# Early rows from six groups, weight loads in the attention's buffers, doubled branch hints and earlier gather conditions in a fused attention and mixture-of-experts kernel

## Chip, cores, metric

The kernel runs on one core of a Trainium2 chip. The metric is the time of one execution in device microseconds (us). Names of engines are those of the profile: PE multiplies matrices, DVE, ACT and POOL work on vectors, SP issues transfers; PEld is PE's weight load.

## The reference

Three stages follow each other. 3072 tokens of 384 numbers each (4 x 768 positions, 8 heads of 48) go through a linear attention with a decaying state; a feed-forward layer of width 2048 with a leaky ReLU follows; then a second mixture of experts, where a token whose skip score is positive goes to the one of 8 experts with the largest logit:

```python
def _moe_ref(x, w_in, w_out):
    h = x @ w_in
    g = np.maximum(0.01 * h, h)
    return (g @ w_out).astype(np.float32)

def _moe2_ref(x, w_skip, w_gate, w1, w2):
    do_compute = x @ w_skip > 0
    out = x.copy()
    xc = x[do_compute]
    logits = xc @ w_gate
    e_idx = np.argmax(logits, axis=1)
    ...                                   # gate_w: softmax weight of the chosen expert
    for e in range(E):
        mask = e_idx == e
        h = np.maximum(xc[mask] @ w1[e], 0.0)
        y[mask] = gate_w[mask, None] * (h @ w2[e])
    out[do_compute] = xc + y
```

How many tokens an expert gets depends on the data: 13, 424, 67, 318, 34, 229, 22 and 69 of experts 0 to 7 here. The kernel works in blocks of 128, so expert 1 has four blocks, expert 3 three, expert 5 two, all others one: 14 blocks.

## The kernel before, in words

Every product is made of three half-precision products (high by high, high by low, low by high part).

**First feed-forward layer.** 3072 tokens are eight groups of 384 (three tiles of 128). For each group the first matmul (`mm1`, L470 to L472) runs over f = 0 to 15, each f giving 128 of the 2048 hidden numbers; ACT and DVE (L475, L476, L485, L486) make the activation and its two halves. Then the second matmul (`mm2`, L498 to L500) makes the output of three tiles. Beside the matmuls of a group the generator `routing` of the group before is advanced at chosen values of f: logits, choice, position of each token in its expert's list, and three scatters by POOL (L592) that write token numbers into three lists in memory, `idxl`. `store_x` writes the finished rows into `xbuf`, from which experts gather them.

**Last group.** The largest expert, E0 = 1, begins early: a first block of 128 of its tokens, the early block, is gathered before all tokens are counted. `early_list` clears the block's buffer, loads the first 128 entries of the three lists (`early_l`, L635, issued by SP), takes the minimum on DVE (L639), gathers the rows by POOL (L653) and transposes them by a transfer of SP (L667). In the last group it runs at f = 7, 8, 11 and 14, the gather limited to rows of the first seven groups. After the last f the attention's pools are closed, buffers `xg` are cleared by POOL (L881) and eight pieces of expert 2's weights, 384 KB each, are loaded (`load_expert`, L691) into `wb`. Pieces are split into halves by ACT and DVE (L188, L189) while the second matmul runs. `counts` reads the counts and the lists back (`h<-idxl`), takes their minimum (L610, L611), transposes it on PE (L615), and puts the counts into registers.

**Experts.** The early block is computed first, then experts 0 to 7. A block is `hidden` (72 short matmuls, L972 to L974, with L978 and L979 on ACT and DVE) and `combine` (24 matmuls of 384 columns, L986 to L988, y on DVE L990, and a scatter into the output by POOL L993). Block j > 0 of an expert stands under a condition on its count (L1071), nested, so that the first block that isn't needed is jumped over with all behind it. Every engine has its own copy of these branches. `announce` places hints for such a branch ahead of it (L1158): for the other engines at the start of a block, for PE after `hidden`. At the start of an expert e stand conditions around the gathers of its further blocks (L1032, L1034) and of the next expert's block 1 (L1041); before expert 1's remaining blocks these are L1037 and L1041. PE executes the branch of each condition, with nothing in it.

Instructions of an engine run in the order in which they stand in its queue.

Of the kernel before, what the change touches and what calls it, by code (L numbers as in the profile page):

```python
# [18 lines left out]
P = 128  # L19
# [5 lines left out]
ST = 128  # L25
# [30 lines left out]
NBLK = 4  # L56


@with_exitstack
def kernel(ctx: ExitStack, tc: tile.TileContext, rk, nat, wT, uN, w_in, w_out, wsg,  # L60
# [15 lines left out]
    raw = ph1.enter_context(tc.tile_pool(name="raw", bufs=3))  # L76
# [39 lines left out]
    def att_load():  # L116
        i = state["loads"]
        assert i < 3 or done["r"] > i - 3
        state["loads"] += 1
        rkt = raw.tile([112, 2, NPAIR, ST], F32, name="rkt")  # L120
        nt = raw.tile([P, 3, 2, NPAIR, D], F32, name="nt")
        sp.dma_start(rkt, rk[i])
        sp.dma_start(nt, nat[i])
        steps[i] = (rkt, nt)

    pw = cst.tile([112, 7, 2, NPAIR], F32, name="pw")
# [496 lines left out]
    def early_list():  # L625
# [14 lines left out]
        gather(E0, 0, None, idx, NT - GT)  # L640
# [193 lines left out]

    rts = iter(())
# [5 lines left out]
    for g in range(NG):  # L841
# [11 lines left out]
        if g > 1:  # L853
            for f in range(NF):
# [7 lines left out]
                if f in ((2, 4, 6) if last else (3, 6, 9)):  # L862
                    next(rts, None)
                if f == (7 if last else 12):
                    for i in range(TPG):
                        store_x(g - 1, i)
                if last and f == 7:
                    firsts = early_list()
                if last and f in (8, 11, 14):
                    next(firsts)  # L870
        if last:
# [4 lines left out]
            w_b = [m2p.tile([P, 768], F32, name=f"wb{i}") for i in range(NW)]  # L876
# [10 lines left out]
            later = [(e, c) for e in range(2, E) for c in range(8)]  # L887
            parts = [load_expert(*later.pop(0), w_b, NW) for _ in range(8)]

            def load_pieces(n):  # L890
                for _ in range(min(n, len(later))):
                    parts.append(load_expert(*later.pop(0), w_b, NW))

            def split_pieces(n, more=True):
                for _ in range(min(n, len(parts))):
                    parts.pop(0)()
                    if more and not state["hold"]:
                        load_pieces(1)
# [59 lines left out]
    def fetch(e, j, k=None, ix=None):  # L958
        gather(e, j, k, ix)
        turn_rows(e, j, k)  # L960

    def hidden(e, k, par, hset, cuts=(0, 0)):
# [3 lines left out]
        for b in range(2):  # L966
# [12 lines left out]
            v.scalar_tensor_tensor(hl, hp, 0.0, hh, op0=ALU.max, op1=ALU.subtract)  # L979

# [32 lines left out]

    def passage():
        turn_here(0, 0, bank[0])
        next(cnts)
        with tc.If(rv[E0] > P):
            fetch(E0, 1)
        with tc.If(rv[0] > P):
            fetch(0, 1)  # L1020
        state["hold"] = False
        load_pieces(4)
# [7 lines left out]
    for e in range(E):  # L1030
        if e != E0:
            with tc.If(rv[e] > 2 * P):  # L1032
                fetch(e, 2)
                with tc.If(rv[e] > 3 * P):  # L1034
                    fetch(e, 3)
        else:
            with tc.If(rv[e] > 3 * P):  # L1037
                fetch(e, 3)
        if e + 1 < E:
            k = 2 if e + 1 == E0 else 1  # L1040
            with tc.If(rv[e + 1] > k * P):  # L1041
                fetch(e + 1, k)
        odd = 1 if e == E0 else 0
        if e == E0:
            fetch_ahead(e + 2)
            split_pieces(sum(PIECES[e + 1]))
        else:
            announce(e, 1)
            cuts = PIECES[e + 1]
            hidden(e, buf_of(e, 0), e % 2, e % 2, cuts[:2])  # L1050
            split_pieces(cuts[2])
            announce(e, 1, ENGINES[:1])
            combine(e, buf_of(e, 0), e % 2, idx_t[:, 0, e:e + 1], lambda: fetch_ahead(e + 2))
        st = ExitStack()
        for j in range(1, NBLK):
            st.enter_context(tc.If(rv[e] > j * P, label=f"e{e}b{j}"))
            announce(e, j + 1)
            hidden(e, buf_of(e, j), (e + j + odd) % 2, 2 if j % 2 else e % 2)
# [103 lines left out]
```

## Time and profile before

| | |
|---|---|
| runs | 662.57, 663.7, 666.19 us |
| median | 663.7 us |
| profiled execution, its own time | 667.2 us |
| its span, first to last instruction | 665.4 us |
| mean granted PE clock | 0.974 |
| PE busy | 613.0 us, 92% of the span |
| DVE, ACT, POOL busy | 422.6, 256.7, 251.4 us |

PE is busy nearly throughout, so the time is read from the gaps between its matmuls: the list of waits says how long, and for whom; the timeline of an engine gives start, duration, operation and, in brackets, the idle time before it and what ended that. Records of branches and hints carry a q behind the engine's name, as PEldq, and belong to its sequencer.

### The profile page before, as it was taken

The page shows a single profiled execution, that of the slowest core. Times are in us where ns is not written, and L with a number is a line of the kernel's source. Part 1 is how long each engine was busy: PE and PEld are TensorE (multiplying, and loading weights), DVE is VectorE, ACT ScalarE, POOL GpSimd, SP SyncE. Part 2 cuts the span into 40 slices and gives each one's busy share as a digit, 9 for nine tenths or more (in the row PEclk, how much of TensorE's full clock was granted, in tenths as well). Part 3 has the DMA queues.
Part 4 walks back from the last instruction along what each step waited for, and adds up shares of the span by engine and source line. Part 5 has one row for each costly group of instructions (what it writes and reads, how often), then busy time and mean ns, then how long its engine had stood idle before and what let it go on. Part 6 is the DMA issues. An engine that isn't in the chain of part 4 may idle for free.

```text
span 665.4 us, 17739 instructions
## 1 busy us (share of the span) xinstructions
PE 613.0 (92%) x7198; PEld 408.5 (61%) x7198; DVE 422.6 (64%) x917; ACT 256.7 (39%) x539; POOL 251.4 (38%) x242
## 2 busy tenths in 40 slices
PE   8879988889999999999999999999969889897984
PEld 5656655556666666666666665665645767675763
DVE  7899988954289469838957934841755362643751
ACT  1225756552144236324434512531534341432530
POOL 2857664443545442633544543110233112311200
PEclk9889999999999999999999999999999899997987
DMA  8757354613626542652642530031239397394740
GB/s 277 219 165 214 82 185 135 184 65 73 168 77 143 158 152 81 159 175 81 140 146 76 112 116 18 2 84 34 72 93 316 108 243 199 91 279 109 209 102 11
DMA packets 60351, 89.06 MB, mean 134 GB/s; under 512 B 20706, under 2 KB 44224, under 8 KB 60240
## 3 DMA queue, kind: packets, MB, share of 16 engines
q1 hardware_dynamic: 56784, 81.64, 43.5%
q0 software_dynamic: 2880, 5.49, 2.8%
q8 instruction: 67, 1.10, 0.7%
q14 instruction: 44, 0.36, 0.2%
q10 hardware_dynamic: 576, 0.47, 0.2%
HBM read 68.86 MB, written 17.23 MB: 129 GB/s over the span
## 4 chain that ended last, share of the span: by engine, by line
PE 41%; DMA 19%; issue 18%; DVE 12%; POOL 5%; ACT 2%; SPq 0%; POOLq 0%; ACTq 0%; DVEq 0%
DMA out_x<-y,idx 10%; PE bank L498 6%; PE bank L500 6%; PE bank L499 6%; DMA idxl<-tokid,su 5%; PE bank L470 5%; PE bank L472 5%; PE bank L471 5%; DMA out_x<-y,early_i 3%; PE bank L399 2%; DVE gg L476 2%; DVE wc L207 2%; PE bank L351 1%; PE bank L327 1%; DVE bank L199 1%
## 5 line engine op out<-in xcount | busy, mean ns | idle before, releaser
L470 PE MATMUL bank<-xt,slotA 128*128 128x384 f16 x384 | 126.0, 328 | 2.4 <-DVE gg L476 2.3
L471 PE MATMUL bank<-xt,slotA 128*128 128x384 f16 x384 | 125.7, 327 | 0.0
L472 PE MATMUL bank<-xt,slotA 128*128 128x384 f16 x384 | 125.7, 327 | 0.0
L498 PE MATMUL bank<-slotB,slotC 128*128 128x393 f16 (+1 forms) x336 | 111.4, 332 | 0.0
L499 PE MATMUL bank<-slotB,slotC 128*128 128x393 f16 (+1 forms) x336 | 111.1, 331 | 0.0
L500 PE MATMUL bank<-slotB,slotC 128*128 128x393 f16 (+1 forms) x336 | 111.1, 331 | 0.0
L476 DVE TENSOR_TENSOR gg<-bank,gg 128x384 f32<-128x384 f32 x128 | 70.0, 549 | 28.7 <-ACT gg L475 28.2
L475 ACT ACTIVATE gg<-bank 128x384 f32<-128x384 f32 x128 | 62.1, 490 | 49.4 <-PE bank L472 46.1
L486 DVE TENSOR_TENSOR slotC<-gg,slotC 128x384 f16<-128x384 f32 x101 | 77.7, 773 | 0.2
L291 POOL TENSOR_TENSOR dg<-cs,diag 128x512 f32<-128x512 f32 x21 | 22.2, 1059 | 132.0 <-DVE cs L284 132.0
L485 ACT CAST slotC<-gg 128x384 f16<-128x384 f32 x112 | 56.8, 508 | 25.3 <-DVE gg L476 25.3
L526 DVE SCALAR_TENSOR_TENSOR x<-bank,x 128x384 f16<-128x384 f32 x24 | 13.2, 556 | 69.6 <-ACT x L523 68.4
L263 POOL TENSOR_TENSOR rkt<-rkt,consts 112x512 f32<-112x512 f32 x44 | 56.9, 1318 | 0.0
L592 POOL DMA_INDIRECT idxl<-tokid,su x24 | 25.5, 1063 | 75.8 <-DVE su L589 65.7
L471 PEld LDWEIGHTS <-slotA 128*128 128x128 f16 x384 | 37.7, 98 | 25.2 <-issue 3.4
L472 PEld LDWEIGHTS <-slotA 128*128 128x128 f16 x384 | 37.7, 98 | 25.2 <-issue 0.5
L470 PEld LDWEIGHTS <-slotA 128*128 128x128 f16 x384 | 37.6, 98 | 24.0 <-issue 0.3
L522 ACT ACTIVATE x<-bank 128x384 f16<-128x384 f32 x24 | 11.8, 492 | 93.2 <-PE bank L500 75.2
L500 PEld LDWEIGHTS <-slotC 128*128 128x128 f16 x336 | 33.1, 98 | 23.2 <-issue 0.7
L498 PEld LDWEIGHTS <-slotC 128*128 128x128 f16 x336 | 33.0, 98 | 22.2 <-issue 0.5
L499 PEld LDWEIGHTS <-slotC 128*128 128x128 f16 x336 | 33.0, 98 | 21.0 <-issue 0.5
L978 ACT ACTIVATE h<-bank 128x512 f16<-128x512 f32 x28 | 16.7, 596 | 72.9 <-PE bank L974 60.6
(213 smaller groups left out, 1319.9 us busy)
## 6 DMA issues: line engine op xcount, KB each, us to landing
wb<-in_w SPq DMA_DIRECT2D x48, 384.0 KB, 6.9
nt<-in_nat SPq DMA_DIRECT2D x24, 576.0 KB, 5.8
rkt<-in_rk SPq DMA_DIRECT2D x24, 448.0 KB, 3.9
xbuf<-x SPq DMA_DIRECT2D x23, 384.5 KB, 4.4
wst<-in_w_in SPq DMA_DIRECT2D x16, 384.0 KB, 9.4
wst<-in_w_out SPq DMA_DIRECT2D x16, 384.0 KB, 3.2
wst<-in_w SPq DMA_DIRECT2D x16, 384.0 KB, 8.0
out_x<-x SPq DMA_DIRECT2D x24, 192.0 KB
```

Source lines behind the costliest of these rows:

```text
L263: eng.tensor_mul(r4[:, a], r4[:, a], tab.unsqueeze(2).broadcast_to([112, NPAIR, 2, C]))
L470: pe.matmul(ph[:, :n], wh, xt[:, 0, k, t0:t0 + n], start=k == 0, stop=False)
L471: pe.matmul(ph[:, :n], wh, xt[:, 1, k, t0:t0 + n], start=False, stop=False)
L472: pe.matmul(ph[:, :n], wl, xt[:, 0, k, t0:t0 + n], start=False, stop=k == NK - 1)
L475: act.activation(gg[:, :n], ph[:, :n], AF.Copy, scale=0.01)
L476: v.tensor_max(gg[:, :n], ph[:, :n], gg[:, :n])
L485: act.copy(gT[:, 0, f, t0:t0 + n], gg[:, :n])
L486: eng.tensor_sub(gT[:, 1, f, t0:t0 + n], gg[:, :n], gT[:, 0, f, t0:t0 + n])
L498: pe.matmul(po[:, :c1 - c0], gh, w_out_s[:, 0, f, c0:c1], start=start, stop=False)
L499: pe.matmul(po[:, :c1 - c0], gh, w_out_s[:, 1, f, c0:c1], start=False, stop=False)
L500: pe.matmul(po[:, :c1 - c0], gl, w_out_s[:, 0, f, c0:c1], start=False, stop=stop)
L592: g_.indirect_dma_start(out=idxl[i], out_offset=bass.IndirectOffsetOnAxis(ap=su[:, i:i + 1], axis=0), in_=tokid[:, ti:ti + 1], in_offset=N ...
```

## The change

1. The attention's input buffers become one lasting tile `raw`; after the attention its slices serve as the weight buffers `w_b`. `load_pieces(1)` stands at every odd f of the last group, and the eight loads after the last f are gone.
2. `early_list` starts at f = 0 of the last group, with steps at f = 1, 3 and 6; the gather is limited to the rows of the first six groups. Steps of `routing` and `store_x` of the group before stand at the same f as in the other groups (3, 6, 9 and 12 instead of 2, 4, 6 and 7).
3. The conditions for the gathers of an expert's blocks 1 and 2 form `fetch_more(e)`. It stands in block 0 of the expert before, between `hidden` and `combine`; for expert 2 it stands ahead of expert 1's block 1, and for the experts 1 and 0 in `passage` of the early block. Block 3's condition stands at the start of block 1.
4. PE's hint is placed twice: after the first half of `hidden` and after `hidden`.

```diff
+RAW = 2 * NPAIR * (ST + 3 * D)
...
-        rkt = raw.tile([112, 2, NPAIR, ST], F32, name="rkt")
-        nt = raw.tile([P, 3, 2, NPAIR, D], F32, name="nt")
+        b = i % 3 * RAW
+        rkt = raw[:112, b:b + 2 * NPAIR * ST].rearrange("p (x a t) -> p x a t", x=2, t=ST)
+        nt = raw[:, b + 2 * NPAIR * ST:b + RAW].rearrange("p (k q a d) -> p k q a d", k=3, q=2, d=D)
...
+    raw = cst.tile([P, 3 * RAW], F32, name="raw")
...
-        gather(E0, 0, None, idx, NT - GT)
+        gather(E0, 0, None, idx, NT - 2 * GT)
...
+    w_b = [raw[:, i * 768:(i + 1) * 768] for i in range(NW)]
...
-                if f in ((2, 4, 6) if last else (3, 6, 9)):
+                if f in (3, 6, 9):
                     next(rts, None)
-                if f == (7 if last else 12):
+                if f == 12:
                     for i in range(TPG):
                         store_x(g - 1, i)
-                if last and f == 7:
+                if last and f == 0:
+                    assert done["r"] == NST
                     firsts = early_list()
-                if last and f in (8, 11, 14):
+                if last and f in (1, 3, 6):
                     next(firsts)
+                if last and f % 2:
+                    load_pieces(1)
...
-            w_b = [m2p.tile([P, 768], F32, name=f"wb{i}") for i in range(NW)]
...
-            parts = [load_expert(*later.pop(0), w_b, NW) for _ in range(8)]
...
+            if between and b == 0:
+                between()
...
+    def fetch_more(e):
+        with tc.If(rv[e] > P):
+            fetch(e, 1)
+            with tc.If(rv[e] > 2 * P):
+                fetch(e, 2)
...
-        with tc.If(rv[E0] > P):
-            fetch(E0, 1)
-        with tc.If(rv[0] > P):
-            fetch(0, 1)
+        fetch_more(E0)
+        fetch_more(0)
...
-        if e != E0:
-            with tc.If(rv[e] > 2 * P):
-                fetch(e, 2)
-                with tc.If(rv[e] > 3 * P):
-                    fetch(e, 3)
-        else:
-            with tc.If(rv[e] > 3 * P):
-                fetch(e, 3)
-        if e + 1 < E:
-            k = 2 if e + 1 == E0 else 1
-            with tc.If(rv[e + 1] > k * P):
-                fetch(e + 1, k)
...
         if e == E0:
+            fetch_more(e + 1)
             fetch_ahead(e + 2)
...
-            hidden(e, buf_of(e, 0), e % 2, e % 2, cuts[:2])
+            hidden(e, buf_of(e, 0), e % 2, e % 2, cuts[:2], lambda: announce(e, 1, ENGINES[:1]))
             split_pieces(cuts[2])
             announce(e, 1, ENGINES[:1])
+            if e + 1 < E and e + 1 != E0:
+                fetch_more(e + 1)
...
+            if j == 1:
+                with tc.If(rv[e] > 3 * P):
+                    fetch(e, 3)
             announce(e, j + 1)
-            hidden(e, buf_of(e, j), (e + j + odd) % 2, 2 if j % 2 else e % 2)
+            hidden(e, buf_of(e, j), (e + j + odd) % 2, 2 if j % 2 else e % 2, (0, 0),
+                   lambda: announce(e, j + 1, ENGINES[:1]))
             announce(e, j + 1, ENGINES[:1])
```

Three places show where instructions stand. The first is SP's queue in the last group: `out_x<-x` are the previous group's output rows, `xbuf<-x` its rows for the experts, `consts<-consts` the transpose of the early block. Before:

```order
L534 DMA out_x<-x_6179 128x384
L541 DMA xbuf<-x_6056 128x769
L541 DMA xbuf<-x_6137 128x769
L541 DMA xbuf<-x_6179 128x769
L635 DMA early_l<-idxl_58 128x1
L635 DMA early_l<-idxl_59 128x1
L635 DMA early_l<-idxl_60 128x1
L667 DMA_TRANSPOSE consts<-consts 128x6x128
L691 DMA wb_6563<-in_w 128x3x256
```

Now:

```order
L536 DMA out_x<-x_6129 128x384
L637 DMA early_l<-idxl_58 128x1
L637 DMA early_l<-idxl_59 128x1
L637 DMA early_l<-idxl_60 128x1
L693 DMA raw<-in_w 128x3x256 x3
L669 DMA_TRANSPOSE consts<-consts 128x6x128
L693 DMA raw<-in_w 128x3x256
L693 DMA raw<-in_w 128x768 x2
L543 DMA xbuf<-x_6006 128x769
L543 DMA xbuf<-x_6087 128x769
L543 DMA xbuf<-x_6129 128x769
```

The list loads and six of eight weight loads stand ahead of the previous group's rows for the experts.

The second is PE's queue from the last matmul of expert 1 to the first of expert 2. Before:

```order
L988 MATMUL bank_95<-slotE,h_6593 128x384
L1064 REGISTER_ALU
L1064 COMPARE_AND_BRANCH
L1064 UNCONDITIONAL_BRANCH
L1061 UNCONDITIONAL_BRANCH
L1071 UNCONDITIONAL_BRANCH x3
L1032 COMPARE_AND_BRANCH
L1034 COMPARE_AND_BRANCH
L1034 UNCONDITIONAL_BRANCH x2
L1032 UNCONDITIONAL_BRANCH
L1041 COMPARE_AND_BRANCH
L1041 UNCONDITIONAL_BRANCH x2
```

Now (L1078 is the condition that was L1071, L1068 the one that was L1061):

```order
L996 MATMUL bank_92<-slotE,h_6542 128x384
L1071 REGISTER_ALU
L1071 COMPARE_AND_BRANCH
L1071 UNCONDITIONAL_BRANCH
L1068 UNCONDITIONAL_BRANCH
L1078 UNCONDITIONAL_BRANCH x3
L978 LDWEIGHTS slotA
```

The conditions for gathers are gone from this place. They stand, as L1023 and L1025, in PE's queue between the hidden layer (L978 to L980 now) and the second matmul (L994) of a block 0, here of expert 2, with the second of the two hints (L1165) ahead of them. Now:

```order
L980 MATMUL bank_90<-xT_6521,slotA 128x128
L1018 ISA
L1165 BRANCH_PREFETCH_HINT
L1023 COMPARE_AND_BRANCH
L1025 COMPARE_AND_BRANCH
L1025 UNCONDITIONAL_BRANCH x2
L1023 UNCONDITIONAL_BRANCH
L994 LDWEIGHTS h_6541
```

The third is PE's queue around the hints for the exit of expert 3, in its last block. Before, the hint stands behind the hidden layer and 24 matmuls ahead of the branch L1071:

```order
L974 MATMUL bank_93<-xT_6578,slotA 128x128
L1010 ISA
L1158 BRANCH_PREFETCH_HINT
L986 LDWEIGHTS h_6592
```

Now both hints stand in the middle of the hidden layer, since nothing holds the second one back:

```order
L980 MATMUL bank_85<-xT_6536,slotA 128x128
L1018 ISA
L1165 BRANCH_PREFETCH_HINT
L978 LDWEIGHTS slotA
L978 MATMUL bank_86<-xT_6536,slotA 128x128
L1165 BRANCH_PREFETCH_HINT
```

The hints stand half a hidden layer, 36 matmuls, further ahead of the branch.

## Rows read from the trace of the kernel before

**Rows 1.** Waits of PE over the span: engine, line, waited for; us in total, times, longest

```profile
PE bank L972 <- PEq L1071: 9.7, 5, 4.9
...
PE bank L569 <- DVE oh L563: 3.5, 1, 3.5
PE bank L972 <- DMA xT<-xg: 3.2, 1, 3.2
...
PE bank L232 <- DVE slotC L486: 2.2, 1, 2.2
...
PE bank L615 <- DVE x L525: 1.0, 1, 1.0
...
PE bank L972 <- DVE xT L663: 0.8, 1, 0.8
```

**Rows 2.** Timeline of DVE, 474 to 498: start, us, line, operation, [idle before]

```profile
481.56 0.55 DVE L486 TENSOR_TENSOR slotC<-gg,slotC 128x384 f16<-128x384 f32 x1
486.47 0.16 DVE L639 TENSOR_REDUCE early_i<-early_l 128x1 uint32<-128x3 uint32 x1 [4.36 <-DMA early_l<-idxl]
...
492.44 3.47 DVE L813 TENSOR_SCALAR lg<-lg 128x27 f32<-128x27 f32 x1
```

**Rows 3.** Timeline of POOL in the same stretch

```profile
491.74 4.14 POOL L881 MEMSET xg<- 128x769 f32 x6 [3.25 <-issue]
```

**Rows 4.** Waits of SP's queue, 460 to 660

```profile
SPq L635 <- DMA idxl<-tokid,su: 6.1, 2, 5.6
```

**Rows 5.** Timeline of DVE, 498 to 535

```profile
519.10 0.68 DVE L611 TENSOR_TENSOR h<-h 8x512 f32<-8x512 uint32 x1 [0.94 <-DMA h<-idxl]
```

**Rows 6.** Windows: us; busy of PE, PEld, DVE, ACT, POOL; clock, DMA share, GB/s

```profile
461.00:485.00 24.00, 24.00 (x213) 15.16 (x211) 14.94 (x47) 12.64 (x29) 3.67 (x4) 1.00 0.19 58
498.00:520.00 22.00, 20.98 (x121) 12.12 (x119) 11.46 (x27) 8.90 (x14) 5.59 (x6) 0.93 0.89 277
```

**Rows 7.** Branch L1071 on PE's sequencer, exits of experts 0, 2, 3, 5: ns min/median/max, start

```profile
L1071 PEldq COMPARE_BRANCH  x1: 4391/4391/4391, 537.8 to 537.8; - x1
...
L1071 PEldq COMPARE_BRANCH  x1: 1398/1398/1398, 574.0 to 574.0; - x1
...
L1071 PEldq COMPARE_BRANCH  x1: 6180/6180/6180, 600.3 to 600.3; - x1
...
L1071 PEldq COMPARE_BRANCH  x1: 3911/3911/3911, 632.9 to 632.9; - x1
```

**Rows 8.** Hints on PE's sequencer, experts 2 and 3

```profile
L1158 PEldq BRANCH_PREFETCH_HINT  x1: 35/35/35, 571.4 to 571.4; - x1
...
L1158 PEldq BRANCH_PREFETCH_HINT  x1: 35/35/35, 597.7 to 597.7; - x1
```

**Rows 9.** Timeline of PE, first matmul of experts 2, 3, 4, 6, 7

```profile
568.26 0.23 PE L972 MATMUL bank<-xT,slotA 128*128 128x128 f16 x1 [1.07 <-DVEq L1061]
...
577.45 0.23 PE L972 MATMUL bank<-consts,slotB 128*128 128x128 f16 x1 [1.09 <-PEq L1071]
...
607.54 0.29 PE L972 MATMUL bank<-xT,slotC 128*128 128x128 f16 x1 [4.90 <-PEq L1071]
...
637.76 0.29 PE L972 MATMUL bank<-xT,slotE 128*128 128x128 f16 x1 [2.55 <-PEq L1071]
...
647.77 0.23 PE L972 MATMUL bank<-consts,slotA 128*128 128x128 f16 x1 [0.47 <-PEq L1071]
```

**Rows 10.** Gather conditions on PE's sequencer over the span: ns min/median/max, first and last

```profile
L1032 PEldq COMPARE_BRANCH  x7: 70/217/337, 530.3 to 647.5; - x7
...
L1041 PEldq COMPARE_BRANCH  x10: 70/186/214, 530.7 to 637.5; - x10
```

**Rows 11.** Windows, columns as in rows 6

```profile
607.60:613.50 5.90, 5.90 (x57) 5.90 (x58) 1.18 (x2) 1.33 (x2) 1.04 (x1) 0.50 0.17 53
637.40:640.80 3.40, 3.04 (x29) 3.04 (x30) 1.32 (x2) 0.00 (x0) 0.00 (x0) 0.50 0.29 75
```

**Rows 12.** The page's DMA queues: packets, MB, share

```profile
q8 instruction: 67, 1.10, 0.7%
```

More of the change, by code (lines that the diff above doesn't have):

```diff
@@ L75 @@
     stg = ph1.enter_context(tc.tile_pool(name="stg", bufs=2))
-    raw = ph1.enter_context(tc.tile_pool(name="raw", bufs=3))
     att = ph1.enter_context(tc.tile_pool(name="att", bufs=2))
@@ L833, in first_logits, with load_pieces, split_pieces @@
         take_logits(0, pl, 1.0 / (SX * SR))
+    w_b = [raw[:, i * 768:(i + 1) * 768] for i in range(NW)]
+    later = [(e, c) for e in range(2, E) for c in range(8)]
+    parts = []
+    def load_pieces(n):
+        for _ in range(min(n, len(later))):
+            parts.append(load_expert(*later.pop(0), w_b, NW))
+    def split_pieces(n, more=True):
+        for _ in range(min(n, len(parts))):
+            parts.pop(0)()
+            if more and not state["hold"]:
+                load_pieces(1)
     rts = iter(())
@@ L861 @@
                     late_logits(g, gT, f - 3, bank[3])
-                if f in ((2, 4, 6) if last else (3, 6, 9)):
+                if f in (3, 6, 9):
                     next(rts, None)
-                if f == (7 if last else 12):
+                if f == 12:
                     for i in range(TPG):
                         store_x(g - 1, i)
-                if last and f == 7:
+                if last and f == 0:
+                    assert done["r"] == NST
                     firsts = early_list()
-                if last and f in (8, 11, 14):
+                if last and f in (1, 3, 6):
                     next(firsts)
+                if last and f % 2:
+                    load_pieces(1)
         if last:
@@ L886 @@
             y_b = [m2p.tile([P, DM], F32, name=f"y{i}") for i in range(2)]
-            later = [(e, c) for e in range(2, E) for c in range(8)]
-            parts = [load_expert(*later.pop(0), w_b, NW) for _ in range(8)]
[L890 to L898, printed above, removed]
         if g == 0:
@@ L960, in fetch, with hidden @@
         turn_rows(e, j, k)
-    def hidden(e, k, par, hset, cuts=(0, 0)):
+    def hidden(e, k, par, hset, cuts=(0, 0), between=None):
         w1s, _ = ev[e % len(ev)]
```

## The prediction

> **What bounds the kernel now.** I read three things in order: which engine is always occupied, what interrupts it, and what the interruptions wait for. PE is the engine; the list of its waits [rows 1] names every idle time that matters behind the attention part. Six entries of it lie in the region that the diff touches: 2.2 us before L232 at the end of the last first layer, 3.5 us before L569 shortly after, 1.0 us before L615, 0.8 us behind L663, and then, between experts, 9.7 us in five waits put down to PE's own sequencer and 3.2 us put down to xT. So the end of the kernel is PE's work plus these gaps, and the change is worth what it takes out of them. Half-speed stretches of PE's clock come on top: two of them [rows 11] hold 5.90 and 3.04 us of PE work at a granted 0.50, which at full speed would be 2.95 and 1.52 us.
>
> The 2.2 us: DVE finishes L486 at 481.56 + 0.55 and then stands 4.36 us before L639, the minimum over the three lists, waiting for the early_l loads [rows 2]. Everything of the running first layer is queued behind L639 on DVE. SP in its turn had waited 5.6 us at L635 for the scatter into idxl [rows 4]. PE runs on from banks that are full already and feels 2.2 of the 4.36.
>
> The 3.5 us are another thing: the tiny scaling L813 took 3.47 us [rows 2] while POOL cleared six xg buffers in 4.14 us from 491.74 [rows 3]. Both stand in the changed program where they stood, so I leave this gap alone.
>
> The gaps between experts: every exit is a branch that jumps over blocks not needed, and the sequencer's record says how long each took [rows 7]: 1.4 us at the end of expert 2, but 4.39 at expert 0, 6.18 at expert 3 and 3.91 at expert 5. The sequencer runs ahead of the matmuls, so 1.4 us disappears and the larger ones don't: PE stood 4.90 us before expert 4 and 2.55 before expert 6 [rows 9], and 3.2 before expert 1 [rows 1]. (Expert 0's is put down to the transfer of xT by the inference of the view; its 4.39 us branch ends at 542.2, two us after the last matmul, and carries it.) Where the branch came in time there is still 1.07, 1.09 and 0.47 us [rows 9]: after the jump PE's sequencer works through the conditions for the next gathers, of which PE executes nothing: 0.07 to 0.34 us each, medians 0.217 at L1032 and 0.186 at L1041 [rows 10].
>
> **The change part by part. Early list.** Its loads now come at f = 1, directly behind the previous group's output stores, and read lists that the group before that had finished; the scatter that SP waited for has left the path. L639 moves up to f = 3, two steps of the loop behind its loads. Of the 4.36 us that DVE stood, most was the scatter that SP had waited for [rows 2, 4]; what is left is the loads' own way. What is queued behind the minimum on DVE is the same chain of L476 and L486, so a late load would cost there what it costs now; I see none. The rows of the last two groups are outside the early gather's bound, and the gather and the transpose leave from f = 3 and 6; SP waits for the gather at the transpose and holds up only loads that nobody needs yet. Gain: 2.2 us, the whole entry of [rows 1]. Bounds: 0, if DVE waits at the new place instead, and 2.2.
>
> **Eight weight loads earlier.** The buffers are the attention's inputs, long unused, so the eight loads of 384 KB leave in the first layer, where the DMA engines are busy 0.19 of the time, instead of in the second matmul, where they are busy 0.89 [rows 6]. They cost nothing where they land: PE doesn't read there and the share is low. What they give: the count chain (scatters, reading back h<-idxl, L610, L611) ran through the crowded stretch, and its last link L611 stood for h<-idxl at 519.10 [rows 5], while the second matmul had ended 1.0 us before L615 began. That the chain speeds up by more than 1 us over its two transfers is likely when some 3 MB leave its window. Gain 1.0 us; bounds 0 and 1.0 + 0.8, the next entry (L663, the rows of expert 0's first block, which come through a store and a gather after the last matmul); I take 1.0 since that second chain does not start sooner.
>
> **Gather conditions sooner.** Counting the branches that stand on PE after the exits of experts 1 to 6: six of L1032, seven of L1041, and two of L1034, which have the same form. Three of the 15 are not taken, at the least value of 0.07 us, and the other twelve I put at 0.2 [rows 10]: 12 x 0.2 + 3 x 0.07 = 2.6 us. All of them go to the place between the hidden layer and the second matmul of a block 0, where the queue of matmuls hides them: for expert 2 the hint that stands there was issued at 571.4 [rows 8], while the block's matmuls ran from 568.26 to 576.36 (577.45 less the gap of 1.09) [rows 9] and the hidden layer, 72 short matmuls, is about half of it, until 572.2; so the sequencer is 0.8 us ahead and meets some 0.3 us of new branches. Uncovered, they would give back at most as much as they cost now. At the exit of expert 0 one set is exchanged for another: 0.1. Gain 2.7 us; bounds 0 and 2.7. The remainder of these gaps, 0.25 to 0.45 us (1.09 less four branches, 0.47 less one), stays. POOL's gathers leave a few us sooner, ahead of a scatter that no one waits for. That costs nothing before the end.
>
> **Hint twice.** A hint costs 35 ns [rows 8] and some register work, in the shadow of the same queue: 0; uncovered, 13 x 0.1 = 1.3 us. For the later blocks of an expert both hints stand in the middle of the hidden layer, 36 matmuls or a quarter of a block, 2.0 us, earlier than now; for a first block one stands there and one where it stood. What do 2.0 us buy? At expert 2 hint and end of the branch lie 4.0 us apart (571.4, and 574.0 + 1.4), at expert 3 they lie 8.7 apart (597.7 to 606.4) [rows 7, 8]. If the time counts from the hint, expert 3's gap shrinks by 2.0; if from the branch, by nothing; if the earlier hint makes it an ordinary exit, by about 4.4. For experts 0 and 5 I expect nothing: they were hinted too and took 3.9 to 4.4 all the same. [...] I take 2.0 us for expert 3 and nothing for the rest, with 0 and the full cure as ends.
>
> [...]
>
> **The sum** is 2.2 + 1.0 + 2.7 + 2.0 = 7.9, against the profiled execution of 667.2 us: 659.3. That execution was 3.5 us above the median of the runs, 663.7; I take the difference off the median: 663.7 - 7.9 = 655.8. I forecast no change in the half-speed stretches: they stand behind the gaps of 4.90 and 2.55 us [rows 9, 11], and the first of these, shortened by 2.0, would still be longer than the second.
>
> **The rivals.** (a) The hints add nothing, the rest holds: 663.7 - 5.9 = 657.8. For it: three hinted exits were late all the same.
> (b) The earlier hints cure the three late exits: expert 3 gives 4.4, experts 0 and 5 about 2.1 each, and the half-speed stretches behind them up to 2.95 + 1.5: 663.7 - 5.9 - 8.6 - 4.5 = 644.7, or 649.2 without the clock. [...]
> (c) Slower: two hints, and new branches between the last hint and the exit, undo what one hint did at the exits that are good now (experts 1, 2, 4 and 6). Such an exit then takes 3.9 to 4.4 us instead of 1.4 [rows 7]; about 1 us of slack is hidden, so it costs 1.9 each, 7.6 for four, and with a half-speed stretch of 1.5 us behind each [rows 11] 13.6. That is 663.7 - 5.9 + 7.6 = 665.4 to 671.4. It decides from three exits on without the clock, from two with it. For it: at these exits the hint's effect hangs on something that the trace doesn't show, as experts 0 and 5 tell, and the code between hint and branch changes. Against it: what is added there jumps over two or three instructions.
> (d) The change doesn't do what it says in its early parts: the minimum waits at its new place or the count chain doesn't speed up; the forecast loses up to 3.2 us, 659.0.
>
> **How the numbers follow.** Forecast 655.8: 0.40; (a) 0.26; (b) 0.12; (c) 0.12; (d) 0.10. The range reaches from (b) without most of its clock gain, 648, to 663.5, which leaves out the rest of (b) and (c), under 2 in 10. Half a per cent, 3.3 us, is what can be told from no change; so faster means under 660.4: most of the forecast, of (a) and (d), and all of (b), 0.76; (c) and overlaps of (d) with lost covers leave 0.13 within and 0.11 slower.
>
> **What would show it.** The wait before the matmul that follows the early list is gone, and DVE does not stand at the minimum; no wait before the transposes of the lists; gaps at experts 2, 3, 5 and 7 fall to 0.25 to 0.45 us; the branch of expert 3 ends some 2 us sooner against its last matmul, those of experts 0 and 5 take 3.9 to 4.4 us as before. Wrong it is if the exits of experts 2, 4 and 6 take over 2 us, if L813's twin grows, or if DVE waits at the new reduce.

## The result and the profile after

The changed kernel took 655.86 us (median of 4 runs, 652.55 to 657.15), the kernel before beside it 664.37 us (4 runs): a ratio of 0.9864, 95% interval 0.9817 to 0.9912. The forecast was 655.8. The total came out, but not by its own terms: some of them were paid by something else, and new losses stand in between.

The page of the changed kernel, its profiled execution of 652.55 us:

```profile
span 650.4 us, 17743 instructions
...
PE 607.9 (93%) x7198; PEld 405.1 (62%) x7198; DVE 422.0 (65%) x917; ACT 256.0 (39%) x539; POOL 251.9 (39%) x242
...
q8 instruction: 67, 1.10, 0.7%
```

The two profiled executions lie 14.7 us apart, the medians 8.5. The difference is chance of single executions: a second profile of the kernel before took 658.85 us, a second one of the changed kernel 661.86. So what repeats in both profiles of a kernel is called its own below, and the rest is a reading of one execution.

Waits of PE in the changed kernel, columns as in [rows 1]. L234, L571, L617, L665 and L978 answer to L232, L569, L615, L663 and L972:

```profile
PE bank L978 <- DVEq L1078: 4.0, 1, 4.0
PE bank L978 <- PEq L1078: 3.7, 3, 2.9
PE bank L571 <- DVE oh L565: 3.5, 1, 3.5
...
PE bank L978 <- DVE xT L665: 1.4, 1, 1.4
...
PE bank L978 <- DMA xT<-xg: 0.6, 1, 0.6
...
PE bank L978 <- PEq L1068: 0.4, 1, 0.4
```

L234 and L617 have left the list, L571 stands as it was, the five waits of 9.7 us for PE's sequencer are three of 3.7, and a wait of 4.0 for a counter of DVE is new. From the first matmul behind the wait of 3.5 us to the end, the first profile of the kernel before took 10.1 us more than that of the changed kernel. The gaps ahead of the first matmul of each piece are half of it (us, both from the timeline of PE):

| gap ahead of | before | after |
|---|---|---|
| the transposes of the lists | 1.02 | 0 |
| expert 0 | 0.84 | 1.35 |
| expert 1 | 3.20 | 4.04 |
| expert 1's block 3 | 0 | 0.61 |
| expert 2 | 1.07 | 0.43 |
| expert 3 | 1.09 | 2.86 |
| expert 4 | 4.90 | 0.44 |
| expert 5 | 0.73 | 0.15 |
| expert 6 | 2.55 | 0.44 |
| expert 7 | 0.47 | 0.15 |
| sum | 15.9 | 10.5 |

That is 5.4 us. Most of the rest is PE's own time: it is busy 141.7 us there before and 138.0 after, because half-speed stretches came or went: 15.9 us of it lie at a granted clock of 0.50 before, 9.3 after. The table shows where the time sits in one execution of each, not what the change is worth: in the two second profiles the same gaps add up to 13.8 us before and 13.6 after. Those two are chance extremes: one is the slowest of six runs of the changed kernel, the other quicker than every other run of the kernel before. The timeline of PE in the changed kernel has the gaps in brackets, as [rows 9] did for before:

```profile
536.55 0.27 PE L978 MATMUL bank<-xT,slotE 128*128 128x128 f16 x1 [4.04 <-DVEq L1078]
...
563.22 0.23 PE L978 MATMUL bank<-xT,slotA 128*128 128x128 f16 x1 [0.43 <-PEq L1068]
...
574.17 0.26 PE L978 MATMUL bank<-consts,slotB 128*128 128x128 f16 x1 [2.86 <-PEq L1078]
...
600.02 0.23 PE L978 MATMUL bank<-xT,slotC 128*128 128x128 f16 x1 [0.44 <-PEq L1078]
```

The branch at the exits of experts 0, 2, 3 and 5 on PE's sequencer, columns as in [rows 7]:

```profile
L1078 PEldq COMPARE_BRANCH  x1: 2499/2499/2499, 530.1 to 530.1; - x1
...
L1078 PEldq COMPARE_BRANCH  x1: 5083/5083/5083, 568.9 to 568.9; - x1
...
L1078 PEldq COMPARE_BRANCH  x1: 1280/1280/1280, 597.2 to 597.2; - x1
...
L1078 PEldq COMPARE_BRANCH  x1: 1675/1675/1675, 621.9 to 621.9; - x1
```

Against [rows 7] the exits of experts 0, 3 and 5 are quicker (4.39, 6.18 and 3.91 before), that of expert 2 is slower (1.40 before). The second profiles of both kernels say the same: 3.77, 5.24 and 3.40 against 2.98, 1.58 and 0.49 at the three, 1.15 against 6.04 at expert 2. The early list on DVE in the changed kernel:

```profile
467.82 0.14 DVE L641 TENSOR_REDUCE early_i<-early_l 128x1 uint32<-128x3 uint32 x1
...
487.56 3.47 DVE L815 TENSOR_SCALAR lg<-lg 128x27 f32<-128x27 f32 x1
```

The minimum has no idle time ahead of it (4.36 us in [rows 2]); the scaling beside POOL's clearing takes the same 3.47 us as there.

### The profile page after: what moved, and what is told of

The parts are those of the page before. It is cut to its first block, busy times and chain, and to the rows that moved or that the text cites. A ratio compares the mean times of both kernels' runs of the same rounds, so it can differ in the third digit from the quotient of the medians.

```text
span 650.4 us, 17743 instructions
## 1 busy us (share of the span) xinstructions
PE 607.9 (93%) x7198; PEld 405.1 (62%) x7198; DVE 422.0 (65%) x917; ACT 256.0 (39%) x539; POOL 251.9 (39%) x242
## 5 line engine op out<-in xcount | busy, mean ns | idle before, releaser
L265 POOL TENSOR_TENSOR raw<-raw,consts 112x512 f32<-112x512 f32 x44 | 56.8, 1315 | 0.1
```

Of the source, the lines that this page charges most:

```text
L265: eng.tensor_mul(r4[:, a], r4[:, a], tab.unsqueeze(2).broadcast_to([112, NPAIR, 2, C]))
```

## Experiments

Open after the result: which part made the exits quicker, why expert 2's became slow, and where the 4.04 us before expert 1 come from. In the texts on record A is the reading held when the run was sent, the others its rivals. Ratios are to the kernel before on the same chip, with 95% intervals.

**The changed kernel again.** No edit.

> The changed kernel once more, to tell what recurs from what is chance. In its first profile the exits of experts 3 and 5 were quick (branch 1.28 and 1.68 us), that of expert 2 took 5.08 us in spite of two hints, and DVE held up expert 1's first block by 4.03 us. Theory A (each is a matter of the program): the same four figures within 1 us, 655 to 657 us. Rival (the late exits fall where chance puts them): expert 2's branch under 1.5 us and another one late, the sum of the gaps between experts different by 2 us or more.

658.01 us against 669.03: 0.9845 (0.9802 to 0.9889). Slow again: the exit of expert 2 (6.04 us) and the wait before expert 1, 7.08 us now, which the timeline of PE puts down to loads of weights:

```profile
544.56 0.27 PE L978 MATMUL bank<-xT,slotE 128*128 128x128 f16 x1 [7.08 <-DMA raw<-in_w]
```

Both recur, as do the quick exits of experts 3 and 5, so they belong to the program. Their sizes do not: of the four figures only those of experts 2 and 3 came back within 1 us, as reading A had it for all.

**One hint.** PE's second hint is taken out everywhere; the one behind `hidden` stays.

```diff
-            hidden(e, ..., cuts[:2], lambda: announce(e, 1, ENGINES[:1]))
+            hidden(e, ..., cuts[:2])
-            hidden(e, ..., (0, 0), lambda: announce(e, j + 1, ENGINES[:1]))
+            hidden(e, ...)
```

> The changed kernel with PE's hint only where it was before the change, after the hidden layer. Theory A (the earlier hint cured experts 3 and 5): their gaps return to about 4.9 and 2.5 us and the half-speed stretches behind them with them, +4.4 +2.1 +2.9 +1.5, and expert 2's exit returns to 1.4 us, -2: in all 4 to 9 us slower than the changed kernel, 660 to 665. Rival (the hints' number has no part in it, code that lies elsewhere or chance has): within 1 us of the changed kernel.

656.7 us: 0.9867 (0.9823 to 0.9912), beside 0.9845 with two hints. That it would be 4 to 9 us slower fell; the rival, within 1 us, agrees with the record. In its profile the gap before expert 3 is 0.83 us (2.86 with two hints), before expert 4 1.93 (0.44), before expert 6 0.79 (0.44): what the second hint gives at experts 3 and 5 it takes at expert 2.

**Conditions back.** The gather conditions stand where they stood before the change.

```diff
-        fetch_more(E0)
-        fetch_more(0)
+        with tc.If(rv[E0] > P):
+            fetch(E0, 1)
+        with tc.If(rv[0] > P):
+            fetch(0, 1)
...
+        if e != E0:
+            with tc.If(rv[e] > 2 * P):
+                fetch(e, 2)
...
-            if e + 1 < E and e + 1 != E0:
-                fetch_more(e + 1)
```

> The changed kernel with the gather conditions and their gathers where they were before the change. Theory A: the small branches return to the exits, +2.4 us in all, and the wait of 4.03 us before expert 1's first block, which came from one more transpose and gather ahead of the weight loads in SP's queue, falls to 3 or less, -1 to -3.5 with the half-speed stretch behind it: between 1.5 us faster and 1.5 slower than the changed kernel. Rival (earlier conditions are a plain gain): 2.4 us slower, 658 to 659, the wait before expert 1 unchanged.

660.65 us: 0.9904 (0.987 to 0.9938), some 2.6 to 4 us of the gain gone by the changed kernel's two ratios, though the intervals overlap. Reading A, no more than 1.5 us slower, is missed; the rival's 2.4 us and unchanged wait come nearer. The wait before expert 1 did not fall as expected (3.95 us). The surprise is expert 3's exit: with both hints in place it is slow again. The branch records at the exits of experts 2 and 3 in this kernel:

```profile
L1086 PEldq COMPARE_BRANCH  x1: 3077/3077/3077, 571.0 to 571.0; - x1
...
L1086 PEldq COMPARE_BRANCH  x1: 5822/5822/5822, 598.9 to 598.9; - x1
```

So both hints without the early gathers do not cure expert 3's exit. The windows suggest why: the four us behind that branch, columns as in [rows 6], where the last but one is the share of the transfer engines. In the kernel before:

```profile
600.30:604.30 4.00, 2.35 (x15) 1.18 (x13) 0.62 (x1) 1.51 (x2) 0.66 (x1) 1.00 0.98 152
```

With the conditions back:

```profile
598.90:602.90 4.00, 2.32 (x15) 1.18 (x12) 0.62 (x1) 0.00 (x0) 0.68 (x1) 1.00 0.88 92
```

In the changed kernel:

```profile
597.20:601.20 4.00, 3.56 (x36) 2.40 (x35) 0.93 (x2) 1.58 (x2) 0.62 (x1) 1.00 0.03 8
```

With one hint:

```profile
595.90:599.90 4.00, 2.39 (x15) 1.23 (x13) 0.70 (x2) 0.96 (x2) 0.61 (x1) 1.00 0.08 16
```

Where the engines are full (0.98, 0.88), the branch takes 6.18 and 5.82 us, with one hint or two; where they are free (0.03, 0.08), 1.28 us with the second hint and 3.85 without.

The other profiles show that free engines behind the branch are not enough. Three more kernels of this document have both hints and early gathers and shares of 0.04 to 0.06 behind the branch, and it takes 2.94 us (loads first, block 3 sooner), 3.21 (early list back) and 3.67 (loads first, again). In the last of these the engines are full ahead of the branch (1.03). From the first hint to the branch, in the changed kernel and in the loads first, again (the share can pass 1 in a short window):

```profile
592.60:597.20 4.60, 4.60 (x67) 3.95 (x64) 1.38 (x2) 1.20 (x2) 0.98 (x1) 1.00 0.58 96
```

```profile
593.60:598.20 4.60, 4.60 (x67) 3.95 (x65) 1.39 (x2) 1.19 (x2) 0.99 (x1) 1.00 1.03 292
```

The branch in the second:

```profile
L1078 PEldq COMPARE_BRANCH  x1: 3667/3667/3667, 598.2 to 598.2; - x1
```

The transfers of instructions (queue q8) put all fourteen profiles in order. The view doesn't say which engine a packet serves, so the fetch is matched by its time: the last one before the branch of expert 3 ends starts 2.4 to 3.3 us ahead of that end in every profile. What differs is how long after the first hint it starts:

| kernel | hint ahead of branch | hint to fetch | branch |
|---|---|---|---|
| before, its two profiles | 2.6, 2.5 | 5.5, 5.2 | 6.18, 5.24 |
| one hint | 2.5 | 3.5 | 3.85 |
| changed, its two profiles | 4.6, 4.5 | 3.5, 3.7 | 1.28, 1.58 |
| conditions back | 4.6 | 7.4 | 5.82 |

In the three kernels named ahead of the table the fetch starts 4.4 to 5.6 us after the hint. So in these profiles the earlier hint gave its two us of lead, and what the transfers took from it was the delay of the fetch. The load is not a complete account of that delay: with one hint the engines are full as well (1.19 between hint and branch), and the fetch starts after 3.5 us.

In the kernel before what fills the engines is the weights (six loads of 384 KB leave from 590.5 us on, and queue q1, which carries them, moves 1.79 of the 2.31 MB between 596 and 606), and when these leave depends on SP, which waits for gathers ahead of them in its queue. Its waits at the transposes in the kernel before, 530 to 610 us:

```profile
SPq L667 <- DMA xg<-xbuf,idx: 46.5, 6, 14.8
```

With the conditions back, same stretch:

```profile
SPq L669 <- DMA xg<-xbuf,idx: 41.6, 5, 15.6
```

In the changed kernel, 515 to 600 us (and 6.6 us for a gather into another buffer):

```profile
SPq L669 <- DMA xg<-xbuf,idx: 19.2, 6, 8.2
```

Here gathers that left sooner let SP pass; the last six weight loads ahead of expert 3's exit left 16.6 us before its branch in the changed kernel, 9.7 in the kernel before, and in the changed kernel the instruction fetch found the engines free (share 0.10 from 596.0 to 597.2 us, the fetch at 596.1). That the weights are what delays the fetch is read from these profiles; no run changed the weights alone.

**Loads first.** In `passage` the four loads stand ahead of the gathers' conditions.

```diff
-        fetch_more(E0)
-        fetch_more(0)
         state["hold"] = False
         load_pieces(4)
+        fetch_more(E0)
+        fetch_more(0)
```

> The changed kernel with the four weight loads of the early block ahead of the gather conditions in the program, so that SP issues them before it waits for two gathers. Theory A (expert 0's y stands on DVE behind two weight splits, whose loads SP issued late): the wait before expert 1's first block falls from 4.03 us to about 1.1, what PE's own branch leaves, and the half-speed stretch behind it may go: 2.9 to 4.5 us faster than the changed kernel, 651 to 653. Rival (the transfers are crowded whatever their order, and the gathers now come later): gap at least 3 us, or the wait moves to the xT of expert 1; within 1 us of the changed kernel.

653.04 us: 0.979 (0.9751 to 0.983), by the medians 5 us under the changed kernel beside it, by the ratios 3.7, with intervals that overlap. The chain is read row by row. SP in the changed kernel, first the two transposes that wait for gathers, then the loads:

```profile
525.09 3.36 SPq L669 DMA_TRANSPOSE xT<-xg  x2
529.04 8.23 SPq L693 DMA_DIRECT2D raw<-in_w  x10
```

ACT in the changed kernel makes the first half of each piece (L190), and stands for these loads:

```profile
533.11 1.81 ACT L190 ACTIVATE slotB<-raw 128x768 f16<-128x768 f32 x2 [3.14 <-DMA raw<-in_w]
```

DVE in the changed kernel: two splits (L191) stand 3.02 us for ACT's halves, expert 0's output row L998 is queued behind them, and only then does DVE reach the exit, where it advances the counter that PE waits for:

```profile
530.01 0.96 DVE L191 SCALAR_TENSOR_TENSOR slotB<-raw,slotB 128x768 f16<-128x768 f32 x1
533.99 1.93 DVE L191 SCALAR_TENSOR_TENSOR slotB<-raw,slotB 128x768 f16<-128x768 f32 x2 [3.02 <-ACT slotB L190]
535.84 0.61 DVE L998 SCALAR_TENSOR_TENSOR y<-bank,xg 128x384 f32<-128x384 f32 x1
```

DVE with the loads first:

```profile
530.53 2.70 DVE L191 SCALAR_TENSOR_TENSOR slotB<-raw,slotB 128x768 f16<-128x768 f32 x3
533.15 0.61 DVE L998 SCALAR_TENSOR_TENSOR y<-bank,xg 128x384 f32<-128x384 f32 x1
```

There the loads left at 516.2, the splits run without a gap, and the wait before expert 1 is 1.08 us, as expected. In all five profiles of this document that have the loads first it is 0.97 to 1.08. What made the wait longer than the 3.20 and 2.51 us of the kernel before is not shown by this: with the conditions back, and one gather only ahead of the loads, DVE stands as long.

```profile
535.62 1.83 DVE L191 SCALAR_TENSOR_TENSOR slotB<-raw,slotB 128x768 f16<-128x768 f32 x2 [3.03 <-ACT slotB L190]
```

Part of the gain moved on: the rows of expert 1's block 3 come late now, as PE's waits show.

```profile
PE bank L978 <- DMA xT<-xg: 3.1, 1, 3.1
...
PE bank L978 <- DVEq L1078: 1.1, 1, 1.1
```

**Early list back.** `early_list`, the bound of its gather and the steps of `routing` stand as before the change.

```diff
-        gather(E0, 0, None, idx, NT - 2 * GT)
+        gather(E0, 0, None, idx, NT - GT)
...
-                if last and f == 0:
+                if last and f == 7:
                     firsts = early_list()
-                if last and f in (1, 3, 6):
+                if last and f in (8, 11, 14):
                     next(firsts)
```

> The changed kernel with the early list and the steps of routing where they were (f = 7, 8, 11, 14 and 2, 4, 6, 7; gather bounded by seven groups), weight loads early as changed. Theory A: the wait of 2.24 us behind DVE's minimum comes back and nothing else moves: 2.2 us slower than the changed kernel, ratio to the kernel before 0.988 to 0.990 against 0.985 to 0.986. Rival (with the weight loads in the same stretch the scatter and the list loads land later): a wait of 3 us or more.

661.89 us against 666.93: 0.9929 (0.99 to 0.9957), the largest loss of the single undoings, some 5 us by the ratios. PE's waits there:

```profile
PE bank L977 <- DMA raw<-in_w: 8.4, 1, 8.4
...
PE bank L234 <- DVE slotC L488: 3.1, 1, 3.1
...
PE bank L617 <- DVE x L527: 0.5, 1, 0.5
```

The wait before L234 is back with 3.1 us, more than reading A's 2.24 and as the rival had it; DVE stands 5.25 at the minimum, a short wait returns before L617, and the one before expert 1 is 8.4.

**Loads back.** The eight weight loads stand behind the last f again.

```diff
-                if last and f % 2:
-                    load_pieces(1)
...
+            load_pieces(8)
```

> The changed kernel with the eight weight loads of expert 2 behind the last first layer again, in the attention's buffers; early list as changed. Theory A: the count chain runs through full transfers, the wait of 1.0 us before the transpose of the lists comes back, and about 0.5 us of it is taken from the wait before expert 0: 0.5 to 1 us slower than the changed kernel. Rival (the chain has room enough): no wait there, no difference.

658.98 us against 666.93: 0.9888 (0.9847 to 0.9928), 1.6 to 2.9 us worse than the changed kernel by its two ratios, though the intervals overlap. There is no wait before L617: the theory that it went with the earlier loads falls. It comes with the late list, 0.54 us in the run above and 1.02 with list and loads both late.

**The kernel before, again.** A second profile of it.

> The kernel before once more, for its profile. If late exits belong to the program: experts 0, 3 and 5 take over 3.5 us at the branch, experts 2, 4, 6 under 1.7. If they are chance: others are late.

658.85 us. Its exits at experts 0, 3 and 5 are long again (above; expert 5's 3.40 us is just under the bound expected, expert 6's 1.76 just over its own), the gaps before experts 4 and 6 are 3.96 and 2.10 us.

**Loads first, block 3 sooner.** To the loads first comes the gather of expert 1's block 3 ahead of expert 2's gathers.

```diff
         if e == E0:
+            with tc.If(rv[e] > 3 * P):
+                fetch(e, 3)
             fetch_more(e + 1)
...
-            if j == 1:
+            if j == 1 and e != E0:
```

> The changed kernel with two orders changed: the early block's four weight loads ahead of the gather conditions (which alone left a wait of 1.08 us before expert 1 and made one of 3.06 us before its block 3), and the gather of expert 1's block 3 ahead of expert 2's in the program. Theory A (SP reaches block 3's transpose late because it works through expert 2's and 3's rows first): the 3.06 us fall below 0.5, 1.5 to 4 us faster than with the loads first alone, ratio to the kernel before 0.973 to 0.977. Rival (the gather itself lands late whatever its place): wait above 2 us, ratio 0.979.

656.2 us: 0.9854 (0.9809 to 0.9898); a miss, 0.973 to 0.977 was expected. The wait before block 3 shrank to 0.33 us, that before expert 1 is 0.97, and yet the whole is no better than the changed kernel.

**One hint in later blocks.** Of the two hints that stand side by side in an expert's blocks 1 to 3, the second is taken out; a first block keeps both.

```diff
             hidden(e, ..., (0, 0), lambda: announce(e, j + 1, ENGINES[:1]))
-            announce(e, j + 1, ENGINES[:1])
```

> The changed kernel with one hint instead of two in an expert's later blocks (both stood side by side in the middle of the hidden layer); first blocks keep both. In the changed kernel no instruction fetch followed the hints of expert 2, in five profiles, though the transfer engines were idle at the first of them; the exits of experts 4, 6 and 7, with hints at the same places, were served. Theory B (the second of two hints side by side, at expert 1's last block, is left over and spoils expert 2's): expert 2's branch falls from 4 to 6 us to under 1.5, its gap from 2.5 to 3.8 us to 0.4, 2 to 4 us faster than the changed kernel. Rival (something else about expert 2): still over 3 us, no difference in time.

654.9 us against 667.48: 0.9819 (0.9767 to 0.987), an interval that overlaps the changed kernel's, so the 2 to 4 us are not shown. The branch is as expected. Expert 2's exit, behind a block of expert 1 with one hint now:

```profile
L1077 PEldq COMPARE_BRANCH  x1: 344/344/344, 571.5 to 571.5; - x1
```

0.34 us instead of 5.08 and 6.04. Its hints, and the transfer of instructions (queue q8: packets, MB, share) between 567.8 and 568.2:

```profile
L1164 PEldq BRANCH_PREFETCH_HINT  x2: 30/32/34, 566.8 to 568.8; - x2
```

```profile
q8 instruction: 1, 0.02, 17.4%
```

The fetch begins 1.0 to 1.4 us after the first hint. In the changed kernel the same two hints come at 564.5 and 566.4, with the transfer engines nearly idle between them (0.10), and the fetch is seen between 571.6 and 571.8 alone, 2.7 us into the branch of 568.9:

```profile
L1165 PEldq BRANCH_PREFETCH_HINT  x2: 34/34/35, 564.5 to 566.4; - x2
```

```profile
564.50:566.50 2.00, 2.00 (x40) 2.00 (x37) 1.78 (x3) 1.01 (x2) 0.52 (x2) 1.00 0.10 35
```

```profile
q8 instruction: 1, 0.02, 29.2%
```

With the conditions back the engines were idler still in the 4.5 us ahead of that branch, and there was no fetch either:

```profile
566.50:571.00 4.50, 4.50 (x66) 3.85 (x64) 3.73 (x6) 2.71 (x5) 1.09 (x1) 1.00 0.04 14
```

So a full queue isn't what cost expert 2 its fetch. All eight profiles with the two hints side by side a block earlier show no fetch between the first hint of expert 2 and its branch, with a share of 0.09 or 0.10 in the two us after that hint, and branches of 3.08 to 6.04 us; all three with one hint there and two in expert 2's own block show it 1.0 to 1.2 us after the hint, and branches of 0.34. The pair decides it, as far as these runs go. That the removed hints also move the code behind them is a rival that no run excludes, and why the other exits behind such a pair do not suffer stays open. A pair is not the only way to a slow exit: with one hint everywhere the branch of expert 2 took 3.05 us, its hint 2.6 us ahead, the engines full (0.97) and the fetch 3.2 us after the hint.

```profile
L1077 PEldq COMPARE_BRANCH  x1: 3054/3054/3054, 571.2 to 571.2; - x1
```

**Loads first, one hint in later blocks.**

> The same with the early block's weight loads ahead of its gather conditions. If both gains are real and stand at different places they add: ratio to the kernel before 0.970 to 0.976. If theory B falls: 0.978 to 0.983, as with the loads first alone.

654.65 us against 667.48: 0.9792 (0.9744 to 0.984). The two do not add to 0.970 to 0.976; the ratio is that of the first measurement of the loads first. In its profile expert 2's branch is 0.34 us again, the wait before expert 1's block 3 is 5.64 us, and expert 3's branch takes 4.92.

**Loads first, again, beside these two.**

> The loads first once more, beside the two others on one chip: ratio 0.976 to 0.983 if the first measurement holds, 0.984 to 0.987 if it was no better than the changed kernel.

656.64 us: 0.9829 (0.9781 to 0.9877); the 5 us of the first comparison shrink, the wait before expert 1 is 0.97 again and that before block 3 3.46.

**All three.** Loads first, block 3 sooner and one hint in later blocks.

> The changed kernel with three things the runs pointed to: the early block's weight loads ahead of the gather conditions, the gather of expert 1's block 3 ahead of expert 2's, one hint in later blocks. Each took away its own wait in a profile (before expert 1 4.0 to 1.0 us, before block 3 of it 3.1 to 0.3, before expert 3 2.5 or more to 0.15). If what follows does not take it back: all three short in one profile and ratio to the kernel before 0.970 to 0.977. Rival (they hand the time on to expert 3's exit and its transfers, as the pairs of them did): ratio 0.978 to 0.984, with waits of 2 us or more before experts 3's later blocks or expert 4.

652.9 us against 665.0: 0.9781 (0.9719 to 0.9843), at the edge of the rival's range and not in the 0.970 to 0.977 expected. PE's waits:

```profile
PE bank L978 <- DMA xT<-xg: 2.9, 2, 1.5
...
PE bank L978 <- PEq L1079: 2.2, 2, 1.8
...
PE bank L978 <- DVEq L1079: 1.0, 1, 1.0
```

The 4.0 us before expert 1 and the 2.9 before expert 3 are gone; small waits for rows and one for expert 5's exit (its branch 3.70 us, the gap 1.76) came in their place. It is the lowest ratio of all, but its interval overlaps those of the changed kernel, so that it beats it is not shown.

## Why the prediction was right, step by step

**Early list, 2.2 us: right, too small.** L234 has left the list of waits and DVE does not stand at the minimum. Undone alone it costs some 5 us: the late list also brings the short wait before L617 and was seen with 8.4 us before expert 1, which varies by itself (4.04 and 7.08 in the changed kernel). The sum counted one entry of the list of waits; where the rest of the 5 us comes from is not shown.

**Eight loads, 1.0 us: right in the row, wrong in the cause.** The wait is gone, but without the early loads it stays away as well. What the loads give, some 2 us if anything, lies elsewhere. And the second chain, put down as limiting at 0.8 us, took up to half of the gain: 1.35 us before expert 0 now, 1.13 in the second profile.

**Gather conditions, 2.7 us: right at the exits, and missed beyond them.** Exits that came in time leave 0.15 to 0.44 us, where 0.25 to 0.45 was forecast. "POOL's gathers leave a few us sooner ... costs nothing" is the sentence that failed, on the good side: the gathers held SP (46.5 us before, 19.2 now), SP held the weights, and by the shares above (0.98 before, 0.03 now) these delayed the fetch at expert 3's exit. The gap there is 4.90 us before, 0.44 with both parts, 1.93 with early gathers and one hint, 4.58 with late gathers and both hints: in these profiles the early gathers alone give 3.0 of the 4.5 us, the second hint alone 0.3. The half-speed stretch of [rows 11] behind it is gone too: the granted clock in the block of expert 4 is 1.00, and PE is busy 8.1 us with it, where the stretch of [rows 11] made it 10.9.

```profile
599.60:608.20 8.60, 8.10 (x96) 6.29 (x96) 7.33 (x9) 6.05 (x10) 2.20 (x2) 1.00 0.59 188
```

On the bad side, two gathers in one stretch stand ahead of the weight loads in SP's queue: the loads left 4.6 us after expert 0's first matmul, with the conditions back 2.9 us, in the kernel before about when it began. The prediction said of SP that it holds up "only loads that nobody needs yet", for the early list, and did not follow what is behind the later transposes: the loads, the splits, the row of expert 0, the counter. How much of the wait before expert 1 the second gather itself adds stays open, since 3.95 us of it were there with the conditions back.

**Hint twice, 2.0 us for expert 3: the lead right, the net wrong.** With early gathers the second hint goes with a gap before expert 4 of 0.44 us instead of 1.93. The fetch starts 3.5 us after the first hint in both, so here the time counts from the hint, as the two us of lead had it. It is not a fixed gain: in the loads first, again, with both hints, that gap is 1.74. And rival (c) came true at one exit: the gap behind expert 2 is 2.86 us with two hints and 0.83 with one. By the prediction's own sign ("if the exits of experts 2, 4 and 6 take over 2 us") this part was wrong, expert 2's branch took 5.08. Net, one hint or two cannot be told apart (0.9867 and 0.9845). That nothing would change at experts 0 and 5 falls: their branches took 2.50 and 1.68 us, in the second profile 2.98 and 0.49, where 3.9 to 4.4 was forecast.

**No change in the half-speed stretches: wrong in detail.** The ones behind the exits of experts 3 and 5 are gone, with a granted clock of 1.00 in the blocks of experts 4 and 6 (the second of them is missing in the second profile of the kernel before as well: short matmuls there take 0.22 us, 0.31 in the stretch at 0.50). New ones stand at the start of expert 3, behind the gap of 2.86 us (0.50 from 573.9 to 577.3), and in expert 1, behind the wait of 4.04 us (0.50 from 536.4 to 539.8, 0.91 on the mean of the whole row):

```profile
536.50:554.10 17.60, 17.52 (x192) 14.16 (x191) 5.30 (x7) 3.23 (x5) 5.09 (x5) 0.91 0.88 253
```

**The sum.** By the single undoings list, conditions and loads are worth about 5, 3 and 2 us, and the second hint nothing that can be told; only the list's interval lies clear of one of the changed kernel's two. These do not add up to the 8.5 us between the medians. An unforeseen gain at expert 3's exit stands against unforeseen losses before experts 1 and 3. That the total meets the forecast within 0.1 us is luck: the interval of the ratio alone is 6 us wide.

## What to carry to other kernels

When a transfer is moved forward in a queue, follow the queue past it: here weights stood behind transposes for which SP waited 46.5 us in the kernel before and 19.2 in the changed one, and they were delayed or freed with these; who reads them decided the price. At the exits of experts 2 and 3 a late branch went with a late instruction fetch in every profile (at expert 3's it ended 2.4 to 3.3 us after the fetch began); look when the fetch starts, and at the load of the transfer engines from the hint on, before more hints are placed. And undo each part alone: a sum that comes out can hide two terms that were wrong in opposite ways.

## What the runs showed of the hardware

- At expert 3's exit the branch ended 2.4 to 3.3 us after the start of the last fetch before that end, in fourteen profiles, and this fetch started 3.5 to 7.4 us after the hint.
- An exit was slow in two ways that look alike in the list of waits: a fetch that started late after its hint, with full engines (share 0.88 to 0.98 behind the branch: 5.8 to 6.2 us), and a hint that no fetch followed before the branch (share 0.10 after the hint and 0.04 ahead of the branch: 5.1 and 3.1 us).
- At expert 2's exit a fetch that followed the hint in time went with a branch of 0.34 us; with one hint in later blocks the fetch began 1.0 to 1.4 us after the hint. A fetch moved 16 KB (1.10 MB in 67 packets [rows 12]). With idle engines (share 0.04) and no fetch ahead one was seen within 0.5 us of the start of a branch (conditions back, the branch of 3.08 us).
- With two hints side by side in expert 1's last block, no fetch followed the hints of expert 2 before its branch, in eight profiles, and the branch took 3.08 to 6.04 us (5.08 and 6.04 in the changed kernel); with one of them it took 0.34, in three. What does this, no run here shows.
